# Sparse attention and soft mixture of experts on one core: keys and queries as 128 interleaved rows, first keys in one transfer, strided values in 32 and 4 rows

## The chip, the core and the metric

The kernel runs on one core of one Trainium2 chip. The metric is the device time of one execution in microseconds. One core has five engines that run side by side: the tensor engine (PE, with its weight loads shown apart as PEld), VectorE (DVE), ScalarE (ACT), GpSimd (POOL) and SyncE (SP). SP computes nothing here; it issues nearly all DMA transfers, in the order of the program.

## The reference

```python
def _attn_ref(q, k, v):                       # (8, 8, 576, 64) each: batch, head, row, width
    scores = scale * np.matmul(q, k.transpose(0, 1, 3, 2))
    rel = pos[:, None] - pos[None, :]
    mask_local = (rel >= 0) & (rel < 32)
    mask_strided = (rel >= 0) & (pos[None, :] % 32 == pos[:, None] % 32)
    # heads 0 to 3 local, heads 4 to 7 strided
    attn = softmax of the masked scores over the keys
    return np.matmul(attn, v)

def _moe_ref(x, phi, w1, w2):                 # x (4608, 512), phi (512, 32), w1 (8, 512, 1024), w2 (8, 1024, 512)
    logits = x @ phi
    d = softmax over the 4608 rows;  slot_input = d.T @ x
    for e in range(8): slot_out[e] = np.maximum(slot_input[e] @ w1[e], 0) @ w2[e]
    c = softmax over the 32 slots
    return c @ slot_out
```

The output of attention, heads side by side, is x of the second part.

## The kernel before, in words

Each of the 8 batches has 576 rows, of which 512 (rows 64 to 575) make one set; the first 64 rows of all eight batches make a ninth, the auxiliary set (index B in the code), which is worked fifth. In the list SETS the sets are numbered 0 to 8 in the order of work.

A set goes through named steps. **Loads** (issued by SP): LKl and LQl load keys and queries of the four local heads, LKs and LQs those of the strided heads, into four buffers `ld` (`load_kq`). A buffer has 128 rows of two times 512 elements. A row of the source holds 8 neighbouring positions of one head (2 KB). Before the change, one transfer fills 64 rows of `ld`, with two heads side by side in each row; a second transfer on the other 64 rows brings the other two heads. LDr loads the first 8 source rows of each head's keys (the 64 keys in front of the set) into `rest`, one transfer of 16 KB a head. V1 loads the local heads' values (runs of 256 bytes, two transfers), VS the strided heads' values (two transfers, each to 36 rows with two heads of 4 KB). W1, W2 and W3 load one weight tile of 512 KB (128 rows of 4 KB) each, as long as own buffers are left. The auxiliary set loads in more and smaller transfers.

**On the engines:** TlK, TlQ, TsK, TsQ and Tr transpose keys, queries and first keys on PE (8 transposes each, Tr 4); lK, lQ, sK, sQ, lrK and srK copy the results from PSUM into the operands kbl, ql, kbs and qs, and put them in order on the way. SL and SS are the two score products with their masks; mx, sb, ex and sm the softmax (maximum, subtraction, exponential, sum); V20 to V23 shift values on GpSimd; PTl and PTs transpose the probabilities, AVl and AVs multiply with the values, nl, X, XB and their copies bring both halves into rows and columns; LGl and LGs make the logits, kp keeps them in `lall`; bm, dex, dT, z, SI and acc update the running softmax over rows and the slot inputs.

The order is written out by hand in `ASEQ`: each entry is a step, its stage, and for copies the engine (A is ScalarE, D VectorE). In iteration `it`, a step of stage s works on set `it - s`, so the steps of one set are spread over five iterations, and one iteration has steps of up to five sets. PE, ScalarE and VectorE run in exactly this order; SP issues in the order in which the loads stand in it. A transfer into a buffer waits until the last reader of the old contents is done, and SP, which goes in order, holds everything behind it.

When a step is done for the last set, the buffers that it was the last to read become free for further weight tiles (`alias`, `freed`), 18 in all, and a load for one is put into SP's order at that place. After attention (the end of SI and acc of the last set) come the global softmax weights, the slot inputs, the two expert layers (h, so), the combination weights (`emit_c`, `emit_ct`) and the output, while the remaining weight tiles are loaded and the results stored (the tail). `shape_constants` makes the masks in the row order of the scores.

Of the kernel before, what the change touches and what calls it, by code (L numbers as in the profile page):

```python
# [22 lines left out]
G = 16  # L23
# [23 lines left out]
def shape_constants():  # L47
    q = np.arange(128)

    qq = q % 16 * 2 + q // 16 % 2  # L50
# [27 lines left out]
def tile_sparse_attention_soft_moe(  # L78
# [64 lines left out]
    ql = fix.tile([P, 2, 16, 32], F32, name="ql")  # L143
# [17 lines left out]
    def load_kq(b, x, i):  # L161
        for j in range(2):

            dma = nc.scalar if b == SETS[0] and j else nc.sync
            out = ld[x][i][64 * j:64 * j + 64]
            if b < B:
                dma.dma_start(out=out, in_=rows_of((k, q)[i], b, x, j)[AR:PN])  # L167
                continue
            for a in range(2):
                rows = (k, q)[i][:, 4 * x + 2 * a + j].rearrange("b (p n) d -> b p (n d)", n=TN)  # L170
                nc.sync.dma_start(out=out[:, a], in_=rows[:, 0:AR])  # L171

    def rows_of(src, b, x, j):
        return src[b, 4 * x:4 * x + 4].rearrange("(a j) (p n) d -> j p a (n d)", j=2, n=TN)[j]

    def load_rest(b):

        for h in range(H):
            if b < B:
                nc.sync.dma_start(out=rest[AR * h:AR * h + AR], in_=k[b, h].rearrange("(p n) d -> p (n d)", n=TN)[0:AR])  # L180
# [11 lines left out]
    def load_vs(b):  # L192
        rows = vs.rearrange("p j g d -> p j (g d)")
        for a in range(2):
            if b < B:
                nc.sync.dma_start(out=rows[64 * a:64 * a + NI],
                                  in_=v[b, 4 + 2 * a:6 + 2 * a].rearrange("j (i g) d -> i j (g d)", g=G))
                continue
# [15 lines left out]
    def flat(t, pat, lo):  # L214
        return t.rearrange(pat)[:, lo:lo + 1024]
# [5 lines left out]
    alias += [(flat(ql, "p j t x -> p (j t x)", 0), {"SL"}), (flat(qs, "p n x -> p (n x)", 0), {"SS"})]  # L221
# [73 lines left out]
    def eT(b, x, i, y, cp):  # L295
        tp = bt[b][f"t{x}{i}"]
        tv = tp.rearrange("p a (n r) -> p (a n) r", n=4)
        if x == 1 and i == 1:
            cp(out=qs, in_=tv)
# [554 lines left out]
```

## Time and profile before

| | us |
|---|---|
| median of 3 runs (336.19 to 339.99) | 337.16 |
| the profiled execution | 339.14 |
| its span, from first to last instruction | 337.3 |
| PE busy in it | 253.5 |
| VectorE busy | 171.7 |
| ScalarE busy | 134.1 |
| GpSimd busy | 48.3 |

All durations of the trace are from the profiled execution; its mean granted TensorE clock was 0.842 of full speed. Busy time is the time in which an engine had an instruction running. A DMA share of 1 means that the packets' times add up to the length of the stretch on all 16 DMA engines; as packets overlap on an engine it can be above 1.

### The profile page before, as it was taken

How to read it: one execution, taken by the hardware profiler on the slowest of the kernel's cores; microseconds unless marked ns; L12 is line 12 of the kernel's file. 1: busy time of each engine (PE TensorE's matmuls, PEld its weight loads, DVE VectorE, ACT ScalarE, POOL GpSimd, SP SyncE). 2: the span in 40 equal slices, each digit the busy share in tenths (PEclk: the TensorE clock that was granted, in tenths of full speed). 3: DMA queues.
4: the chain of work that ended last, by engine and by line, in shares of the span. 5: the costliest groups of instructions: out<-in, count | busy, mean ns of one | idle time of the engine just before them, and what ended most of it. 6: DMA issues, size and time to landing. Idle time of an engine off the chain costs nothing.

```text
span 337.3 us, 10114 instructions
## 1 busy us (share of the span) xinstructions
PE 253.5 (75%) x4417; PEld 191.4 (57%) x4417; DVE 171.7 (51%) x316; ACT 134.1 (40%) x235; POOL 48.3 (14%) x47
## 2 busy tenths in 40 slices
PE   7467959779996739886986969995645689999820
PEld 2455847568785638575665848774445343357610
DVE  2157836552865424853861745666103126569740
ACT  1356443633574405544544544452301301128620
POOL 8004004004003000500500400400050002000000
PEclk9789978965999967997898797896759559999985
DMA  6979969969968979978996996999999558999997
GB/s 144 213 168 222 211 154 215 213 153 212 188 192 152 149 157 189 209 182 171 219 204 156 213 212 146 230 266 379 189 277 285 174 187 235 350 347 347 324 343 241
DMA packets 65740, 74.36 MB, mean 220 GB/s; under 512 B 24608, under 2 KB 50592, under 8 KB 65696
## 3 DMA queue, kind: packets, MB, share of 16 engines
q1 hardware_dynamic: 64304, 72.45, 89.2%
q10 hardware_dynamic: 1392, 1.26, 1.5%
q8 instruction: 35, 0.57, 0.8%
q14 instruction: 9, 0.07, 0.1%
HBM read 64.26 MB, written 9.44 MB: 218 GB/s over the span
## 4 chain that ended last, share of the span: by engine, by line
DMA 38%; PE 30%; SPq 10%; DVE 9%; issue 4%; ACT 4%; POOL 1%; ACTq 0%; DVEq 0%; POOLq 0%
DMA wb<-in_moe_w_dram 22%; DMA ld<-in_k_dram 12%; PE h L672 5%; PE so L770 4%; SPq L167 4%; DMA v<-in_v_dram 3%; PE t L293 3%; PE as L280 3%; PE o L798 3%; SPq L187 2%; PE al L280 2%; SPq L171 2%; PE ss L280 2%; DVE kbl L309 2%; PE pt L417 1%
## 5 line engine op out<-in xcount | busy, mean ns | idle before, releaser
L293 PE MATMUL t<-ident,ld 128*128 128x128 f32 x288 | 49.4, 325 | 19.4 <-DMA ld<-in_k_dram 11.1
L293 PEld LDWEIGHTS t<-ident,ld 128*128 128x128 f32 x288 | 40.0, 168 | 26.6 <-issue 14.6
L210 POOL COPY v<-v 32x1024 f32<-32x1024 f32 x18 | 19.1, 1061 | 201.9 <-DMA v<-in_v_dram 155.1
L312 ACT COPY ql<-t 64x512 f32<-64x512 f32 x36 | 20.9, 580 | 36.7 <-PE t L293 31.2
L309 DVE COPY kbl<-t 64x512 f32<-64x512 f32 x18 | 12.4, 688 | 32.1 <-PE t L293 27.1
L280 PE MATMUL as<-pt,vs 36*64 36x32 f32 x1152 | 22.7, 234 | 5.8 <-issue 5.5
L280 PEld LDWEIGHTS as<-pt,vs 36*64 36x64 f32 x1152 | 21.2, 152 | 8.3 <-issue 7.8
L280 PEld LDWEIGHTS al<-v,pt 128*32 128x32 f32 x576 | 17.6, 117 | 11.8 <-POOL v L208 7.0
L280 PE MATMUL al<-v,pt 128*32 128x128 f32 x576 | 19.3, 289 | 6.5 <-POOL v L208 6.1
L302 ACT COPY kbs<-t 64x1024 f32<-64x1024 f32 x18 | 18.1, 1007 | 13.7 <-PE t L293 13.6
L309 ACT COPY kbl<-t 64x512 f32<-64x512 f32 x18 | 10.4, 580 | 30.7 <-DVE kbl L309 30.7
L431 DVE TENSOR_TENSOR xn<-al,rz 128x512 f32<-128x512 f32 x18 | 11.6, 685 | 21.3 <-PE al L280 21.3
L542 ACT COPY pt<-pt 128x1024 f32<-128x1024 f32 x9 | 9.1, 1017 | 27.5 <-PE pt L417 27.5
L208 POOL COPY v<-v 32x1024 f32<-32x1024 f32 x18 | 19.4, 1081 | 1.1
L280 PE MATMUL ss<-kbs,qs 128*32 128x72 f32 x576 | 12.5, 232 | 8.9 <-issue 7.0
L280 PE MATMUL lg<-xt,phs 128*32 128x128 f32 x288 | 15.4, 342 | 4.4 <-issue 3.3
L280 PE MATMUL sl<-kbl,ql 128*32 128x128 f32 x576 | 17.8, 276 | 0.6 <-DVE kbl L336 0.6
L280 PEld LDWEIGHTS sl<-kbl,ql 128*32 128x32 f32 x576 | 15.3, 111 | 4.9 <-DVE kbl L336 1.9
L336 DVE COPY kbl<-tr 64x32 f32<-64x32 f32 x24 | 4.4, 185 | 25.6 <-PE tr L322 18.8
L417 PE MATMUL pt<-ident,pl 128*128 128x128 f32 x72 | 15.6, 387 | 2.1 <-issue 2.1
L543 ACT COPY xt<-as 128x1024 f32<-128x1024 f32 x9 | 9.1, 1013 | 19.9 <-PE lg L280 19.7
L280 PEld LDWEIGHTS ss<-kbs,qs 128*32 128x32 f32 x576 | 10.4, 110 | 11.6 <-issue 11.6
(157 smaller groups left out, 447.4 us busy)
## 6 DMA issues: line engine op xcount, KB each, us to landing
wb<-in_moe_w_dram SPq DMA_DIRECT2D x43, 512.0 KB
ld<-in_q_dram SPq DMA_DIRECT2D x30, 256.0 KB
ld<-in_k_dram SPq DMA_DIRECT2D x30, 256.0 KB
v<-in_v_dram SPq DMA_DIRECT2D x16, 288.0 KB
vs<-in_v_dram SPq DMA_DIRECT2D x16, 288.0 KB
out_dram<-wb SPq DMA_DIRECT2D x6, 512.0 KB
ld<-in_moe_w_dram SPq DMA_DIRECT2D x4, 512.0 KB
v<-in_moe_w_dram SPq DMA_DIRECT2D x3, 512.0 KB
```

The lines of the kernel that those rows point to most:

```text
L167: dma.dma_start(out=out, in_=rows_of((k, q)[i], b, x, j)[AR:PN])
L208: nc.gpsimd.tensor_copy(out=v2[r + 32:r + 64, a], in_=v1[r:r + 32, a, :, 1:9])
L210: nc.gpsimd.tensor_copy(out=v2[r:r + 32, a], in_=v1[r + 32:r + 64, a, :, 0:8])
L280: nc.tensor.matmul(out=out, lhsT=lhsT, rhs=rhs, start=start, stop=stop, skip_group_check=True)
L293: nc.tensor.transpose(out=tp[:, a, P * n:P * n + P], in_=src[:, a, P * n:P * n + P], identity=ident)
L302: cp(out=kbs[r, y].rearrange("p n (j r) -> p n j r", j=2)[:, :, :, AR:PN], in_=tv[r].rearrange("p n (j r) -> p n j r", j=2))
L309: cp(out=kbl[d, a, e::2].rearrange("p n (j r) -> p n j r", j=2)[:, :, :, AR:PN], in_=tp[r, a].rearrange("p (n j r) -> p n j r", n=4, j=2))
L312: cp(out=ql[d, :, :, 16 * e:16 * e + 16].rearrange("p j t (r n) -> p (j t) r n", n=4), in_=tp[r, a].rearrange("p (n t r) -> p t r n", n=4, ...
L417: nc.tensor.transpose(out=ps[:, g // 4, 128 * (g % 4):128 * (g % 4) + 128], in_=(pl[:, 2 * g:2 * g + 2] if x == 0 else psd[:, g]).rearrang ...
L431: nc.vector.tensor_tensor(out=xn[:, :, 0:256].rearrange("p r (a j d) -> p j r a d", a=2, j=2)[:, j], in0=bt[b]["al"][:, j].rearrange("p (r ...
L672: nc.tensor.matmul(out=ph[x][32 * e:32 * e + 32, :], lhsT=sit[:, c, 32 * (4 * g + e):32 * (4 * g + e) + 32], rhs=wts[16 * g + 4 * c + e][: ...
L770: nc.tensor.matmul(out=pos[x][32 * e:32 * e + 32, 0:256], lhsT=hts[g][:, c, 32 * e:32 * e + 32], rhs=wt[:, 256 * e:256 * e + 256], start=( ...
```

## The change

Keys and queries: a transfer now takes two neighbouring heads and fills all 128 rows of one half of `ld`, in the order (row, head), so that row p of head j lands in row 2p + j of the buffer. The evacuations read every second column to sort the heads apart; queries of the local heads are laid out 8 neighbouring rows to a group, SL takes every second column of ql as weights, AVs writes its columns in the same new order, and the logits' rows are put into the old order when they are kept (kp, now two copies), so that the copies of `emit_ct` no longer reorder. The masks follow. The first set's second key and query transfers are issued by SP and no longer by ScalarE. The first keys of all eight heads come in one transfer of 128 KB. The strided values of 36 rows come as rows 4 to 35 and then rows 0 to 3. The free buffers other than `ld` are filled with weight tiles only once V1 and VS of the last set are issued. The order of the steps is a new one; the stages are four higher throughout, which changes nothing by itself.

```diff
 ASEQ = (
-    "V23:4 lK3:3A V22:4 lK2:3D lK0:3A LGs:5 TsQ:3 lrK2:3A lrK3:3D sms:4 W1:4 srK1:3A ePTl:4A nms:4 XB:5 srK0:3A "
-    "kp:5 LDr:2 bm:5 LKl:2 dex:5 eXB:5A SL:3 dT:5 alx:5 sQ:3D edT:5D mxl:3 z:5 TsK:3 sK0:3A SI:5 AVl:4 sbl:3 "
-    "sK1:3A PTs:4 ePTs:4A nl0:4 exl:3 nl1:4 SS:3 mxs:3 sbs:3 LQs:2 acc:5 V1:3 X:4 LKs:2 W2:3 TlQ:2 AVs:4 VS:3 "
-    "Tr:2 lQ0:2A LQl:1 lQ2:2A eX:4D V21:3 exs:3 lQ3:2A LGl:4 sml:3 W3:3 lQ1:2A eAVs:4A TlK:2 lrK0:2D lK1:2D "
-    "lrK1:2D V20:3 PTl:3 "
+    "edT:9D mxl:7 sK1:7A SI:9 sbl:7 sK0:7A PTs:8 SS:7 z:9 ePTs:8A W2:7 nl1:8 nl0:8 W3:8 LKl:6 V1:7 V22:7 X:8 "
+    "acc:9 eX:8A V20:7 mxs:7 Tr:6 lrK0:6A TlK:6 sbs:7 exl:7 lK0:6D lK2:6D lK3:6A lK1:6D LQl:6 AVs:8 LGl:8 LQs:6 "
+    "PTl:7 lrK1:6D V21:7 TlQ:6 LKs:6 exs:7 lQ2:6D eAVs:8A lrK2:6A ePTl:7A lrK3:6D lQ1:6A lQ3:6A lQ0:6A LGs:8 "
+    "LDr:5 sml:7 TsQ:6 XB:8 sQ:6A V23:7 bm:8 W1:7 sms:7 TsK:6 srK0:6A nms:7 kp0:8A kp1:8A SL:6 dex:8 dT:8 VS:7 "
+    "eXB:8A srK1:6A AVl:7 alx:8 "
...
-    qq = q % 16 * 2 + q // 16 % 2
+    qq = q % 4 * 8 + q // 4 % 4 * 2 + q // 16 % 2
...
     def load_kq(b, x, i):
-        for j in range(2):
-            dma = nc.scalar if b == SETS[0] and j else nc.sync
-            out = ld[x][i][64 * j:64 * j + 64]
+        src = (k, q)[i]
+        for a in range(2):
             if b < B:
-                dma.dma_start(out=out, in_=rows_of((k, q)[i], b, x, j)[AR:PN])
+                rows = src[b, 4 * x + 2 * a:4 * x + 2 * a + 2].rearrange("j (p n) d -> p j (n d)", n=TN)
+                nc.sync.dma_start(out=ld[x][i][:, a], in_=rows[AR:PN])
                 continue
-            for a in range(2):
-                rows = (k, q)[i][:, 4 * x + 2 * a + j].rearrange("b (p n) d -> b p (n d)", n=TN)
-                nc.sync.dma_start(out=out[:, a], in_=rows[:, 0:AR])
+            for j in range(2):
+                rows = src[:, 4 * x + 2 * a + j].rearrange("b (p n) d -> b p (n d)", n=TN)
+                nc.sync.dma_start(out=ld[x][i][j::2, a], in_=rows[:, 0:AR])
...
     def load_rest(b):
-        for h in range(H):
-            if b < B:
-                nc.sync.dma_start(out=rest[AR * h:AR * h + AR], in_=k[b, h].rearrange("(p n) d -> p (n d)", n=TN)[0:AR])
+        if b < B:
+            nc.sync.dma_start(out=rest, in_=k[b].rearrange("h (p n) d -> h p (n d)", n=TN)[:, 0:AR])
...
         for a in range(2):
             if b < B:
-                nc.sync.dma_start(out=rows[64 * a:64 * a + NI],
-                                  in_=v[b, 4 + 2 * a:6 + 2 * a].rearrange("j (i g) d -> i j (g d)", g=G))
+                src = v[b, 4 + 2 * a:6 + 2 * a].rearrange("j (i g) d -> i j (g d)", g=G)
+                for lo, hi in ((4, NI), (0, 4)):
+                    nc.sync.dma_start(out=rows[64 * a + lo:64 * a + hi], in_=src[lo:hi])
...
         if x == 1 and i == 1:
-            cp(out=qs, in_=tv)
+            cp(out=qs.rearrange("p n (j r) -> p n j r", j=2), in_=tv.rearrange("p n (r j) -> p n j r", j=2))
         elif x == 1:
...
-               in_=tv[r].rearrange("p n (j r) -> p n j r", j=2))
+               in_=tv[r].rearrange("p n (r j) -> p n j r", j=2))
...
-                   in_=tp[r, a].rearrange("p (n j r) -> p n j r", n=4, j=2))
+                   in_=tp[r, a].rearrange("p (n r j) -> p n j r", n=4, j=2))
...
-                cp(out=ql[d, :, :, 16 * e:16 * e + 16].rearrange("p j t (r n) -> p (j t) r n", n=4),
-                   in_=tp[r, a].rearrange("p (n t r) -> p t r n", n=4, r=4))
+                cp(out=ql[d, :, 32 * e:32 * e + 32].rearrange("p t (n r) -> p t n r", n=4),
+                   in_=tp[r, a].rearrange("p (n t r) -> p t n r", n=4, r=8))
...
-                    mm(ps[32 * c:32 * c + 32, j, 128 * r:128 * r + 128], ql[:, j, 4 * r + c],
+                    mm(ps[32 * c:32 * c + 32, j, 128 * r:128 * r + 128], ql[:, 4 * r + c, j::2],
...
-        pv = ps.rearrange("p a (c e h g) -> p a e g c h", e=2, h=2, g=8)
+        pv = ps.rearrange("p a (t e c h w) -> p a e w c t h", e=2, c=4, h=2, w=2)
...
-    def kp(b):
-        nc.scalar.copy(out=lall[:, SETS[b], :], in_=bt[b]["lg"][:, 0:128])
+    def kp(b, e, cp):
+        cp(out=lall[:, SETS[b], :].rearrange("p (t r n e) -> p e t r n", r=4, n=4, e=2)[:, e],
+           in_=bt[b]["lg"][:, 0:128].rearrange("p (t e n r) -> p e t r n", e=2, n=4, r=4)[:, e])
...
-                for x in [x for x in alias if x[1] <= done]:
+                for x in [x for x in alias if x[1] <= done and ({"V1", "VS"} <= done or x[0].tensor in first)]:
...
-                CTE[vb % 2](out=dst.rearrange("p (c k e) -> p c k e", e=2, k=16),
-                            in_=src.rearrange("p (c e k) -> p c k e", e=2, k=16))
+                CTE[vb % 2](out=dst, in_=src)
```

`first` is the list of the four `ld` buffers.

## Rows read from the trace of the kernel before

**Rows 1.** The page's first two parts, whole span: busy time, share and instructions of each engine; then, in 40 slices of 8.4 us, the share of the DMA engines in tenths and the bytes they moved.

```profile
PE 253.5 (75%) x4417; PEld 191.4 (57%) x4417; DVE 171.7 (51%) x316; ACT 134.1 (40%) x235; POOL 48.3 (14%) x47
...
DMA  6979969969968979978996996999999558999997
GB/s 144 213 168 222 211 154 215 213 153 212 188 192 152 149 157 189 209 182 171 219 204 156 213 212 146 230 266 379 189 277 285 174 187 235 350 347 347 324 343 241
```

**Rows 2.** The page's fourth part: the chain of work that ended last, by engine.

```profile
DMA 38%; PE 30%; SPq 10%; DVE 9%; issue 4%; ACT 4%; POOL 1%; ACTq 0%; DVEq 0%; POOLq 0%
```

**Rows 3.** The timeline of SP, which issues the loads: start, time of the issue, line, what is loaded, how many. The first key loads of set 1 (local heads) and of set 8, and the three weight tiles that go into ld near the end of attention.

```profile
18.06 1.25 SPq L167 DMA_DIRECT2D ld<-in_k_dram  x2
...
205.04 1.25 SPq L167 DMA_DIRECT2D ld<-in_k_dram  x2
...
220.48 5.13 SPq L257 DMA_DIRECT2D ld<-in_moe_w_dram  x3
```

**Rows 4.** Stretches of the span, one row each: from:to, length, busy time and instructions of PE, PE's weight loads, DVE, ACT and POOL, then the granted TensorE clock, the DMA share and GB/s. In order: one set from key load to key load; 3 us around its start; the same around the start of set 8; keys and queries in flight; the last part of the set; weight tiles in flight; the auxiliary set's key and query loads; the tail.

```profile
43.50:69.40 25.90, 18.34 (x397) 14.90 (x397) 12.31 (x22) 11.56 (x19) 4.14 (x4) 0.87 0.95 195
42.50:45.50 3.00, 2.52 (x132) 2.21 (x131) 2.61 (x4) 2.70 (x5) 0.00 (x0) 1.00 0.18 37
204.50:207.50 3.00, 3.00 (x82) 2.67 (x80) 3.00 (x4) 1.02 (x2) 0.00 (x0) 0.64 0.35 89
46.50:51.50 5.00, 1.82 (x9) 1.82 (x10) 0.00 (x0) 1.01 (x1) 0.00 (x0) 0.50 1.09 215
58.60:69.40 10.80, 7.02 (x159) 5.32 (x158) 5.19 (x8) 5.34 (x7) 0.00 (x0) 1.00 0.89 191
228.00:231.00 3.00, 1.21 (x69) 1.21 (x71) 2.93 (x4) 0.56 (x1) 0.00 (x0) 0.92 1.03 402
92.00:94.00 2.00, 1.84 (x42) 1.59 (x46) 1.21 (x2) 0.66 (x1) 0.00 (x0) 1.00 0.55 196
284.00:304.00 20.00, 20.00 (x253) 9.49 (x242) 12.45 (x40) 4.60 (x12) 0.00 (x0) 1.00 1.09 347
```

**Rows 5.** SP's timeline again, the issues of one set, as in rows 3.

```profile
43.84 1.25 SPq L167 DMA_DIRECT2D ld<-in_k_dram  x2
...
49.19 2.92 SPq L167 DMA_DIRECT2D ld<-in_k_dram  x2
52.15 0.60 SPq L257 DMA_DIRECT2D wb<-in_moe_w_dram  x1
52.84 0.75 SPq L196 DMA_DIRECT2D vs<-in_v_dram  x2
...
55.21 2.13 SPq L257 DMA_DIRECT2D wb<-in_moe_w_dram  x2
58.67 10.91 SPq L180 DMA_DIRECT2D rest<-in_k_dram  x8
69.68 1.27 SPq L167 DMA_DIRECT2D ld<-in_k_dram  x2
```

**Rows 6.** The DMA queue's own waits: what SP waited for at line 180 (loads of the first keys), total us, times, longest.

```profile
SPq L180 <- DMA wb<-in_moe_w_dram: 27.4, 17, 3.6
SPq L180 <- DMA vs<-in_v_dram: 17.8, 12, 2.6
```

**Rows 7.** Stretches as in rows 4: the densest 20 us of attention, and all of it up to the end of the last SI.

```profile
80.00:100.00 20.00, 19.35 (x430) 16.05 (x428) 14.04 (x24) 11.89 (x22) 3.69 (x4) 0.91 0.80 199
0.00:269.40 269.40, 203.59 (x3905) 163.30 (x3905) 135.38 (x224) 113.70 (x187) 46.43 (x45) 0.84 0.92 202
```

**Rows 8.** Groups of instructions by line and shape: line, engine, operation, out<-in, shapes, count | busy us, mean ns of one | idle time before them and what ended it. The query and key evacuations of the local heads, the weight loads of the two score products, and the copy of the logits.

```profile
L312 ACT COPY ql<-t 64x512 f32<-64x512 f32 x36 | 20.9, 580 | 36.7 <-PE t L293 31.2 <-DMA ld<-in_k_dram 5.1
...
L280 PEld LDWEIGHTS sl<-kbl,ql 128*32 128x32 f32 x576 | 15.3, 111 | 4.9 <-DVE kbl L336 1.9 <-issue 1.7 <-DVE rz L408 0.8
...
L309 ACT COPY kbl<-t 64x512 f32<-64x512 f32 x18 | 10.4, 580 | 30.7 <-DVE kbl L309 30.7
L280 PEld LDWEIGHTS ss<-kbs,qs 128*32 128x32 f32 x576 | 10.4, 110 | 11.6 <-issue 11.6
...
L495 ACT COPY lall<-lg 128x128 f32<-128x128 f32 x9 | 2.4, 264 | 1.2 <-PE lg L280 1.2
```

**Rows 9.** The chain of work followed back, at the start: start us, us, what.

```profile
2.28 4.74 DMA ld<-in_q_dram
...
7.35 5.92 DMA ld<-in_k_dram
...
13.32 1.98 PE t L293 x8
```

**Rows 10.** The same chain in the last set and after it.

```profile
210.11 1.95 PE t L293 x8
...
233.03 11.33 DMA v<-in_v_dram
...
248.87 3.74 PE al L280 x64
252.61 1.91 PE pt L417 x8
...
269.39 0.76 DVE acc L514
...
292.49 0.86 PE so L770 x16
```

More of the change, by code (lines that the diff above doesn't have):

```diff
@@ L142, in tile_sparse_attention_soft_moe @@
     kbl = fix.tile([P, 2, TN, RW], F32, name="kbl")
-    ql = fix.tile([P, 2, 16, 32], F32, name="ql")
+    ql = fix.tile([P, 16, 64], F32, name="ql")
     kbs = fix.tile([P, 2, 8, RW], F32, name="kbs")
@@ L161, in load_kq @@
     def load_kq(b, x, i):
-        for j in range(2):
-            dma = nc.scalar if b == SETS[0] and j else nc.sync
-            out = ld[x][i][64 * j:64 * j + 64]
+        src = (k, q)[i]
+        for a in range(2):
             if b < B:
-                dma.dma_start(out=out, in_=rows_of((k, q)[i], b, x, j)[AR:PN])
+                rows = src[b, 4 * x + 2 * a:4 * x + 2 * a + 2].rearrange("j (p n) d -> p j (n d)", n=TN)
+                nc.sync.dma_start(out=ld[x][i][:, a], in_=rows[AR:PN])
                 continue
-            for a in range(2):
-                rows = (k, q)[i][:, 4 * x + 2 * a + j].rearrange("b (p n) d -> b p (n d)", n=TN)
-                nc.sync.dma_start(out=out[:, a], in_=rows[:, 0:AR])
-    def rows_of(src, b, x, j):
-        return src[b, 4 * x:4 * x + 4].rearrange("(a j) (p n) d -> j p a (n d)", j=2, n=TN)[j]
+            for j in range(2):
+                rows = src[:, 4 * x + 2 * a + j].rearrange("b (p n) d -> b p (n d)", n=TN)
+                nc.sync.dma_start(out=ld[x][i][j::2, a], in_=rows[:, 0:AR])
     def load_rest(b):
-        for h in range(H):
-            if b < B:
-                nc.sync.dma_start(out=rest[AR * h:AR * h + AR], in_=k[b, h].rearrange("(p n) d -> p (n d)", n=TN)[0:AR])
+        if b < B:
+            nc.sync.dma_start(out=rest, in_=k[b].rearrange("h (p n) d -> h p (n d)", n=TN)[:, 0:AR])
     def load_v1(b):
@@ L220, in tile_sparse_attention_soft_moe @@
              for x in range(2) for i in range(2)]
-    alias += [(flat(ql, "p j t x -> p (j t x)", 0), {"SL"}), (flat(qs, "p n x -> p (n x)", 0), {"SS"})]
+    alias += [(flat(ql, "p t x -> p (t x)", 0), {"SL"}), (flat(qs, "p n x -> p (n x)", 0), {"SS"})]
     alias += [(flat(t, "p e n r -> p (e n r)", x), {n}) for t, n in ((kbl, "SL"), (kbs, "SS")) for x in (0, 1024)]
@@ L446, in AVs @@
                             o = 128 * (2 * e + w) + 32 * c
-                            mm(pv[64 * j:64 * j + 64, a, e, 4 * w + c], vs[d, j, 8 * w + 2 * c + e], pt[d, j, o:o + 32])
+                            mm(pv[64 * j:64 * j + 64, a, e, w, c], vs[d, j, 8 * w + 2 * c + e], pt[d, j, o:o + 32])
     def X(b):
@@ L533, in tile_sparse_attention_soft_moe @@
         "LGl": lambda b: LG(b, 0), "LGs": lambda b: LG(b, 1), "nl0": lambda b: nl(b, 0), "nl1": lambda b: nl(b, 1),
-        "bm": bm, "dex": dex, "alx": alx, "kp": kp, "dT": dT, "z": z, "SI": SI,
+        "bm": bm, "dex": dex, "alx": alx, "dT": dT, "z": z, "SI": SI,
         "acc": lambda b: emit_acc(slice(0, 512), bt[b]["si"], bt[b].get("al_")),
@@ L538, in tile_sparse_attention_soft_moe @@
     moves = {
+        "kp0": lambda b, cp: kp(b, 0, cp), "kp1": lambda b, cp: kp(b, 1, cp),
         "sQ": lambda b, cp: eT(b, 1, 1, 0, cp),
@@ L557, in tile_sparse_attention_soft_moe @@
     done = set()
+    first = [t.tensor for t in ld[0] + ld[1]]
     for it in range(min(x[1] for x in todo), NV + max(x[1] for x in todo)):
```

## The prediction, made before the change was run

> **What bounds the kernel now.** I began with the whole span: tensor engine 75% busy, VectorE and ScalarE about half, the DMA share six to over nine tenths in the first 24 slices (202 us), yet only 144 to 222 GB/s there against about 345 near the end [rows 1]. The chain that ended last is 38% DMA and 10% SP's own issuing [rows 2]. So the larger part of the run waits for loads, and the question is why they are slow there. The unit to look at is one set (one batch's 2.1 MB of keys and queries, 0.13 MB of first keys, 0.59 + 0.59 MB of values, three weight tiles of 0.52 MB, 4.97 MB together). The key loads of set 1 were issued at 18.06 us and those of set 8 at 205.04 [rows 3]: seven sets in 187.0 us, 26.7 us each.
>
> Inside one set I read SP's issues beside the byte rates, and three things show. (1) While only keys and queries move, the rate is 215 GB/s although the DMA share is over 1; where weight tiles alone were queued (the three into ld and those around them), with 128 rows instead of 64, it is 402 GB/s at the same share [rows 3, 4]. The queues are full in both, so I read the 64-row destination as what halves the rate. (2) In the last 10.8 us of the set, which hold two strided value loads, one pair of query loads, two weight tiles and the eight small loads of the first keys, it is 191 GB/s [rows 4]. At their own rates the queries take 2 x 262 KB / 215 = 2.4 us and the two weight tiles 2 x 524 KB / 402 = 2.6; of the 10.8 some 5.8 us are left for the two value loads of 295 KB, 2.9 us each where a weight tile of nearly twice the bytes takes 1.3. (3) The first keys take SP 10.91 us for eight issues of 16 KB [rows 5], since each is held until an earlier load has landed [rows 6]. The last one therefore goes out when everything else is home, and the next keys behind it: in the 3.0 us around that point the rate is 37, in another set 89 GB/s, at DMA shares of 0.18 and 0.35 [rows 4].
>
> The pieces of a set: keys and queries 8 x 1.22 = 9.8 us, strided values 5.8, local values 0.59 MB at the 191 to 215 around them 2.9, weights 3 x 1.30 = 3.9, the hole 3.0 us less what its shares say was busy, 2.0 to 2.5. That is 24.4 to 24.9 of the 25.9 us from one key load to the next, close enough to cost an edit by its piece.
>
> The next bound is the tensor engine. Up to the last SI the trace has 3905 matmuls, 12 of them warm-ups; by nine that is 433 a set [rows 7]. The densest stretch ran 430 in 19.35 us at a granted clock of 0.91 [rows 7]; so 19.5 us a set, with idle time on top.
>
> **The change, part by part.**
>
> *Keys and queries, 128 rows to a transfer.* Same bytes, same eight issues, 2 KB runs as before. If (1) is right they go from 215 to the rate of 128-row loads. Bounds: 215 (no gain, 9.8 us) and 402 (5.2 us). I take 380, for a 2 KB run is half a weight row: 5.5 us, 4.3 less. [...]
>
> *Strided values, 32 + 4 rows.* Two loads become four. The 32 rows are meant to go evenly; the 4 rows carry a ninth of the bytes. Bounds: 5.8 us as now, and 1.5 us at 402. I take 3.0, nearer the lower, since (1) says that the spread of rows is what counts.
>
> *First keys in one transfer.* Removes seven issues a set (23 become 18 with the two extra for values) and, what matters, the hole: one transfer waits for one landing, and later loads queue behind it at once. The transfer is eight heads of 16 KB; the nearest row is the auxiliary set's 128 KB loads, also eight pieces, at 196 GB/s and a share of 0.55 [rows 4]: 0.7 us. The hole of 2.0 to 2.5 us goes. But the new order has waits of its own on SP: V1 for AVl of the set before, at the end of PE's round, with LQl, LQs and LKs behind it; LDr for Tr, with one weight tile and VS behind; VS for AVs, with two weight tiles and the next LKl behind. For a restart after V1's wait I keep 1.5 us (bounds 0 and 3.0).
>
> DMA per set after: 5.5 + 3.0 + 2.9 + 3.9 + 0.7 + 1.5 = 17.5 us (all low ends 14.2; all high ends 26.1). That is below PE's 19.5, so what is late next is PE. With 1.3 us of waits on evacuations and late loads I take 20.4 us for a common set. The auxiliary set stays at 128 KB transfers, sixteen of them at 196: 10.7 instead of 5.5 us, DMA 22.7, so 23 for this one. Mean of seven: (6 x 20.4 + 23) / 7 = 20.8 us (bounds 19.5, PE without a wait, and 26.1, all high DMA ends at once).
>
> *The evacuations that sort.* Reads of every second element from PSUM: the query copies already read in steps and take 580 ns, as the key copies in longer runs do, same size [rows 8]. Nothing, on engines with 12 to 14 us of work in a set [rows 7]. Moving qs and xt to ScalarE and two 64-row copies back keeps both under 15; cover is PE's 19.5. kp becomes two copies, bounded by 0 and one more of 264 ns [rows 8], off the path. Weight loads of every second column of ql: ss already loads so, 110 ns against 111 for sl [rows 8]: nothing. AVs' scattered output columns: no row has a two-column step alone; bounds 0 and a few tenths of a us; I take 0. The closing copies without a step lie beside a tail whose DMA share is 1.09 at 347 GB/s [rows 4]: nothing.
>
> *Start.* Now PE's first key transposes begin at 13.32 us, released by a key load issued at 7.35 behind the first keys [rows 9]. All of set 0's loads then go over SP, 0.6 us an issue for 262 KB as now [rows 3]. One transfer and two key loads, 0.66 MB, come first; ScalarE's query load, issued at 2.28 among others, was home 4.74 us later [rows 9]; a key load issued at 1.5 in the same crowd is there at 6 us (bounds 4.8 and 10.3). Less 7.3.
>
> *Last set.* Now V1 of set 8 sits on SP behind weight tiles that fill freed buffers: issued at 233.03, 11.33 us to land, and AVl starts at 248.87 [rows 10]. From set 8's key transposes (210.11) to the end of the last SI (269.4) it is 59.3 us. Afterwards only the tiles into ld go ahead; the others wait for V1 and VS. At the new pace: 15.5, three quarters of 20.4, for the rest of set 8's round; 3 for LQl and LKs, which now stand on SP behind ld tiles that wait for TlK and TlQ; 15.5 again for the next round, which has no key and query transposes and no sl; 17 for the closing chain (now from AVl's end, 252.6, to 269.4): 51 us (bounds 46 and 59). The eleven tiles now held back cost 11 x 1.3 = 14 us of DMA, first needed by so at 292.49, 23 us after SI [rows 10]: covered; without that cover it would be up to 14 us.
>
> *Tail.* From acc to the end, 67.9 us, full of DMA and PE, is left alone (bounds -1, +3).
>
> **The sum.** Now 13.3 + 9.8 (to set 1's place) + 187.0 + 59.3 + 67.9 = 337.3. After: 6 + 9.8 + 7 x 20.8 + 51 + 67.9 = 280.3. The profiled execution took 339.14, 1.84 more than its span, and the median of the runs is 0.994 of it: (280.3 + 1.84) x 0.994 = 280.5, so 280 us.
>
> **The rivals.**
>
> *A: the rate stays at that of 64 rows.* What speaks for it: no load in the trace pairs a 128-row destination with a source of 64 rows by two heads, and the slow rate could come from the 2 KB runs. Against: the auxiliary loads have 2 KB runs too and give 196 GB/s at half the share. [...] Time: 4.3 us more DMA a set, 21.8 + 1.3 = 23.1, with slower start (8) and end (54): 8 + 9.8 + 161.7 + 54 + 67.9 = 301.4, 301 us.
>
> *B: the hole comes back at V1.* SP waits in order; V1 for AVl, and TlQ, TsQ, TsK then need LQl, LQs, LKs within the first half of PE's round. For: the strided heads' key loads, issued next after V1, held SP for 2.92 us where a free pair takes 1.25 [rows 5]. Against: LKl is ahead of V1, and six loads at 0.7 us are quick. If PE stands 3 us a set, 23.8: 280.3 + 21 = 301 us.
>
> *C: slower, fewer engines.* A transfer whose source steps between two heads may be spread over few engines, as the share of 0.55 hints for the auxiliary set's eight pieces [rows 4]. Price: with x GB/s for 2.1 MB, a set is slower than 26.7 once keys and queries take 26.7 - 12.0 = 14.7 us, below 143 GB/s. At a quarter of 196 they take 43 us, a set 55, and the run 530 us. The auxiliary loads, eight pieces at 196, speak against falling that far.
>
> **How the numbers follow.** Forecast 0.64, A 0.16, B 0.14, C 0.03, and 0.03 for other outcomes near today's time (a later wait eats all). The range takes in 19.5 us a set with the best start and end (5 + 9.8 + 136.5 + 46 + 67 = 264) and A and B at 301, with half of their 21 us again to spare for the size of either: 264 to 312. The three runs of before lie within 1.1%, so about 1% is what can be told from no change. Faster by over 1%: 0.64 + 0.16 + 0.14 + 0.01 = 0.95; within 1% 0.02; slower 0.03.
>
> **What would show it.** In the trace after: stretches of key and query loads alone above 340 GB/s (A: near 215); one first-key issue a set, of under a us, and no 3 us stretch under 100 GB/s between sets; a set of 20 to 21.5 us with PE busy over 90%, clock near 1; first key transposes near 6 us; set 8's V1 issued right after the AVl before it; 68 us from the last SI to the end. Wrong if PE idles for loads in every set (B), if the clock drops below the 0.91 of the dense stretch (1 us more a set per 5%), or if the tail grows since the held-back tiles are late.

## The result, and the profile after

The changed kernel takes 287.83 us (median; 287.54 to 290.65), the kernel before 337.58 beside it: a ratio of 0.854, with a 95% interval of 0.847 to 0.861. Predicted were 280, with a range of 264 to 312. The profiled execution has a span of 285.6 us where the sum said 280.3. Here and below, ratios leave out executions that are over 1.5% longer than the fastest of the same kernel, medians and ranges do not.

The page of the changed kernel: busy time of the engines; PE's granted clock and the DMA share in 40 slices of 7.1 us; then the chain of work that ended last, by engine.

```profile
PE 238.1 (83%) x4417; PEld 175.3 (61%) x4417; DVE 156.8 (55%) x308; ACT 141.2 (49%) x252; POOL 46.9 (16%) x47
...
PEclk9999789999999975999978699999965699999965
DMA  7999999699878998879979919976999999999997
...
PE 65%; DVE 7%; issue 7%; ACT 7%; DMA 6%; SPq 4%; DVEq 0%; ACTq 0%
```

Against [rows 1, 2]: DMA has gone from 38% of the chain to 6%, SP's own issuing from 10 to 4, PE from 30 to 65. The same matmuls keep PE busy for 15 us less; its mean clock rose from 0.842 to 0.902. The bound has moved, as forecast. But the DMA engines are hardly less busy than before: still at nine tenths in most slices of attention.

The same chain in order of time (start, us, what), which dates each step of the sum: the first key transposes; `sl` of sets 1, 2, 3, 5, 6, 7 and 8 (the auxiliary one is not on the chain); what the chain went through in the auxiliary set; two of PE's pauses ("issue": PE waits for nothing that the profile shows); set 8's key transposes, the AVl of sets 7 and 8, and acc after the last SI.

```profile
5.92 1.19 PE t L289 x8
...
25.14 2.48 PE sl L276 x66
...
50.32 2.32 PE sl L276 x66
...
70.60 2.32 PE sl L276 x66
...
92.64 10.80 DMA ld<-in_k_dram
...
118.18 2.32 PE sl L276 x66
...
136.66 2.32 PE sl L276 x66
...
140.67 2.53 issue
...
153.72 3.17 issue
...
165.20 2.32 PE sl L276 x66
...
174.44 1.02 PE t L289 x8
...
184.45 2.31 PE sl L276 x66
187.03 2.07 PE al L276 x64
...
199.52 1.88 PE al L276 x64
...
217.61 0.76 DVE acc L512
```

From one `sl` to the next: 25.2, 20.3, 47.6 for the auxiliary set and its neighbour together, 18.5, 28.5, 19.3. Three of the five common sets run at or under the 20.4 us forecast for one, the other two don't; the mean of seven is 22.8 instead of 20.8. That is where the prediction was off.

Stretches of the changed kernel, columns as in [rows 4]: seven sets from `sl` to `sl`; keys and queries in flight; the strided values with weight tiles; a set without a pause; the set with two of them.

```profile
25.14:184.29 159.15, 140.22 (x3019) 114.19 (x3019) 90.99 (x164) 91.97 (x155) 28.96 (x28) 0.91 0.90 231
...
40.00:42.00 2.00, 2.00 (x113) 1.83 (x112) 1.36 (x2) 1.17 (x3) 1.88 (x3) 1.00 1.05 389
...
44.00:50.00 6.00, 4.44 (x48) 3.84 (x49) 3.12 (x8) 4.09 (x8) 0.00 (x0) 1.00 1.05 210
...
118.18:136.66 18.48, 18.37 (x434) 15.17 (x433) 13.20 (x25) 13.38 (x25) 4.14 (x4) 1.00 0.84 224
136.66:165.20 28.54, 22.74 (x434) 17.98 (x433) 13.22 (x25) 13.36 (x25) 4.14 (x4) 0.82 0.92 236
```

Keys and queries move at 389 GB/s where [rows 4] had 215. The stretch with the strided values still shows 210 at a DMA share of 1.05. And the first row holds the difference to the forecast: in a set PE is busy for 140.22 / 7 = 20.0 us and idle for 2.7, where the forecast for a common set had 19.5 and 0.9.

What PE waited for in these seven sets (total us, times, longest):

```profile
PE al L276 <- issue: 7.3, 3, 3.4
PE t L289 <- DMA ld<-in_k_dram: 3.7, 2, 2.2
PE lg L276 <- issue: 3.2, 1, 3.2
...
PE t L289 <- DMA ld<-in_q_dram: 0.9, 2, 0.6
```

With 1.5 and 1.0 us before two other steps the pauses make 13.0 of the 18.9 us, the waits for loads 4.6. All of these 4.6 stand in the auxiliary set and its neighbour, between 84.67 and 103.58. In the five common sets PE waited for no load: the one without a pause in the rows above took 18.5 us, the one with two 28.5, 5.7 of it in the pauses and 4.4 more in matmuls at a granted clock of 0.82 instead of 1.00.

SP's timeline (columns as in [rows 3]): the one load of the first keys and the four of the strided values, in one set.

```profile
39.67 0.64 SPq L175 DMA_DIRECT2D rest<-in_k_dram  x1
...
42.54 2.23 SPq L193 DMA_DIRECT2D vs<-in_v_dram  x4
```

And SP's longest wait: total us, times, longest.

```profile
SPq L182 <- PE al L276: 36.4, 7, 9.9
```

0.64 us of SP instead of 10.91 [rows 5]. SP now waits for PE, at V1, 5.2 us a set.

### The profile page after: what moved, and what is told of

Read it like the earlier page. It is cut to its first block, busy times and chain, and to the rows that moved or that the text cites. A ratio compares the mean times of both kernels' runs of the same rounds, so it can differ in the third digit from the quotient of the medians.

```text
span 285.6 us, 10033 instructions
## 1 busy us (share of the span) xinstructions
PE 238.1 (83%) x4417; PEld 175.3 (61%) x4417; DVE 156.8 (55%) x308; ACT 141.2 (49%) x252; POOL 46.9 (16%) x47
## 4 chain that ended last, share of the span: by engine, by line
PE 65%; DVE 7%; issue 7%; ACT 7%; DMA 6%; SPq 4%; DVEq 0%; ACTq 0%
PE t L289 7%; PE sl L276 7%; PE as L276 6%; PE al L276 6%; PE pt L413 6%; PE h L673 5%; PE so L769 5%; ACT ql L308 4%; DMA ld<-in_k_dram 4%; PE ss L276 4%; PE o L797 3%; SPq L170 3%; PE lg L276 3%; PE si L276 3%; PE x L449 3%
## 5 line engine op out<-in xcount | busy, mean ns | idle before, releaser
L289 PE MATMUL t<-ident,ld 128*128 128x128 f32 x288 | 42.9, 288 | 7.9 <-DMA ld<-in_k_dram 4.3
L289 PEld LDWEIGHTS t<-ident,ld 128*128 128x128 f32 x288 | 32.6, 146 | 15.6 <-issue 3.4
L305 DVE COPY kbl<-t 64x512 f32<-64x512 f32 x27 | 18.5, 686 | 19.6 <-PE t L289 13.1
L276 PE MATMUL al<-v,pt 128*32 128x128 f32 x576 | 18.9, 276 | 7.3 <-issue 7.3
L276 PEld LDWEIGHTS al<-v,pt 128*32 128x32 f32 x576 | 15.7, 110 | 9.1 <-issue 8.1
L308 DVE COPY ql<-t 64x512 f32<-64x512 f32 x9 | 6.2, 684 | 24.4 <-PE t L289 24.4
L308 ACT COPY ql<-t 64x512 f32<-64x512 f32 x27 | 15.7, 581 | 5.3 <-DVE ql L308 5.0
L539 ACT COPY xt<-x 128x1024 f32<-128x1024 f32 x9 | 9.1, 1012 | 13.6 <-PE x L449 13.6
L384 DVE TENSOR_REDUCE mx<-sl 128x16 f32<-128x1024 f32 x9 | 11.0, 1217 | 5.3 <-PE sl L276 5.3
L673 PE MATMUL h<-wb,v 128*32 128x512 f32 x104 | 13.8, 637 | 0.0
L276 PEld LDWEIGHTS lg<-xt,phs 128*32 128x32 f32 x288 | 7.7, 114 | 9.9 <-issue 7.5
```

Of the source, the lines that this page charges most:

```text
L276: nc.tensor.matmul(out=out, lhsT=lhsT, rhs=rhs, start=start, stop=stop, skip_group_check=True)
L289: nc.tensor.transpose(out=tp[:, a, P * n:P * n + P], in_=src[:, a, P * n:P * n + P], identity=ident)
L305: cp(out=kbl[d, a, e::2].rearrange("p n (j r) -> p n j r", j=2)[:, :, :, AR:PN], in_=tp[r, a].rearrange("p (n r j) -> p n j r", n=4, j=2))
L308: cp(out=ql[d, :, 32 * e:32 * e + 32].rearrange("p t (n r) -> p t n r", n=4), in_=tp[r, a].rearrange("p (n t r) -> p t n r", n=4, r=8))
L384: nc.vector.tensor_reduce(out=stats(b, "mx", x), in_=scores(b, x), op=ALU.max, axis=AX.X)
L673: nc.tensor.matmul(out=ph[x][32 * e:32 * e + 32, :], lhsT=sit[:, c, 32 * (4 * g + e):32 * (4 * g + e) + 32], rhs=wts[16 * g + 4 * c + e][: ...
```

## The experiments

The theory at the start was the prediction's own: in the old kernel each piece of a set's DMA time is on the path, so each part of the change gives its piece until PE binds. The rival: the DMA engines are the bound as a whole, so that filling a hole gives nothing, and a part counts once another has moved the bound. Times of different experiments are compared through their ratios to the kernel before, which ran beside each. Of four kernels (the rows alone, all but the rows, and in the new kernel the values in 36 rows and the old rule for buffers) only the times are used.

**The first keys in one transfer, alone, in the old kernel.**

```diff
-        for h in range(H):
-            if b < B:
-                nc.sync.dma_start(out=rest[AR * h:AR * h + AR], in_=k[b, h]...[0:AR])
+        if b < B:
+            nc.sync.dma_start(out=rest, in_=k[b].rearrange("h (p n) d -> h p (n d)", n=TN)[:, 0:AR])
```

> The kernel before with one edit: the first keys of all eight heads in one transfer (everything else as before). My theory: the hole of 2.0 to 2.5 us a set, in which nothing is in flight, goes, in seven sets and at the start, where the key load no longer stands behind eight small ones: 337 falls to 314 to 322 us, and the 3 us around a set's first key load move at 150 GB/s or more instead of 37 to 104. Rival (the hole is only moved, since SP goes in order and the next wait takes its place): 330 to 338 us.

Measured 338.48 us, ratio 0.996 (0.990 to 1.001): nothing, though the hole is gone. One set of this kernel, from one set's first key load to the next, columns as in [rows 4]:

```profile
42.26:68.34 26.08, 23.33 (x496) 18.93 (x496) 14.77 (x25) 14.25 (x22) 4.14 (x4) 0.91 1.02 182
```

In this set the share went from 0.95 [rows 4] to 1.02, and the bytes from 195 to 182 GB/s: more packet time, and no more moved. So the 3 us at 37 and 89 GB/s were real, but filling them gained nothing there. Why is not settled. The chain of this run is not that of the kernel before [rows 2]:

```profile
PE 47%; DMA 25%; issue 8%; SPq 6%; ACT 5%; DVE 5%; ACTq 0%; DVEq 0%
```

DMA and SP have fallen from 48% of it to 31, PE and its pauses have risen from 34 to 55. Less was waited for loads, and as much came back in PE's work and pauses.

**The strided values in 32 and 4 rows, alone, in the old kernel.**

```diff
-                nc.sync.dma_start(out=rows[64 * a:64 * a + NI], in_=v[b, ...]...)
+                src = v[b, 4 + 2 * a:6 + 2 * a].rearrange("j (i g) d -> i j (g d)", g=G)
+                for lo, hi in ((4, NI), (0, 4)):
+                    nc.sync.dma_start(out=rows[64 * a + lo:64 * a + hi], in_=src[lo:hi])
```

> The kernel before with one edit: strided values as 32 rows (4 to 35) and 4 rows (0 to 3). My theory (the spread of the rows sets the rate, not the bytes): 2.8 us less DMA a set where DMA is the bound, 337 falls to 312 to 320 us. Rival (value rows cost by their bytes and by the issue, of which there are now two more a set): 335 to 340 us.

333.33 us, ratio 0.984 (0.974 to 0.993): 5.5 us over the run (2 to 9 by the interval), where 2.8 us a set would have been some 20.

**The 128-row keys and queries with what they need, without the other parts.** The old order, first keys, values and rule for freed buffers are kept.

> The kernel after, with the old order of steps, the old eight loads of the first keys, the old 36-row values and the old rule for freed buffers; so of the change only the 128-row keys and queries with the sorting copies are left. My theory: 4.3 us less DMA a set, 337 falls to 298 to 308 us, and keys and queries alone move at 380 to 400 GB/s. Rival (the gain came from the hole and the order): 325 to 335 us.

312.94 us, ratio 0.916 (0.910 to 0.923). Of the change's 49 us (0.146 of 338) the rows give 28 alone.

**All but the 128-row keys and queries.** The new order, first keys, values and rule, with 64-row loads and the old copies.

> The kernel after without the 128-row keys and queries: old 64-row transfers and old copies, with the new order, one transfer for the first keys, 32 + 4 value rows and the new rule for freed buffers. My theory (rival A of the prediction as an experiment): DMA is 4.3 us a set longer, 21.8 us, and again about as long as PE's round: 300 to 306 us. Rival (order and hole did it, the rate of the rows hardly matters): 287 to 293 us.

318.07 us, ratio 0.937 (0.931 to 0.943): the rows are worth 28 us inside the new kernel (0.937 less 0.854, of 338). That is more than the 300 to 306 us that the price of rival A gave.

**The new kernel with one part undone**, four runs. Eight first-key loads:

> The kernel after, with the eight loads of 16 KB for the first keys again. One transfer alone changed nothing in the kernel before, so two readings are open. One: the hole was never worth anything, since the loads around it slow down by as much when it is filled; then 286 to 291 us here. Two: it was worth nothing only while DMA was the bound in every other microsecond of the set; now that PE sets the pace, eight issues that each wait for a landing hold up the loads behind them: 296 to 306 us, with SP's first-key issues at 5 us or more a set.

299.33 us, ratio 0.886 (0.879 to 0.893). The edit that gave nothing in the old kernel is worth 0.032 of 338, 11 us, in the new one. The values in one transfer of 36 rows:

> The kernel after, with the strided values in two transfers of 36 rows again. In the kernel before the split was worth 1.6%, some 0.7 us a set. If the split still only saves DMA time that PE's round now covers: 287 to 290 us. If the values are the loads that a set waits for: 293 to 300 us.

292.13 us (286.16 to 294.41): its fastest run lies under the fastest of the changed kernel, 287.54, so no worth of this part is shown in the new kernel. The old order of steps:

> The kernel after, with the old order of steps (kp in its two halves on ScalarE at the old place); loads as after. If the loads alone made the gain: 287 to 295 us. If the order is needed so that PE does not wait for a load that SP issued late: 302 to 312 us, near the 313 of the 128-row loads alone.

292.68 us, ratio 0.868 (0.859 to 0.877), about 5 us, though the intervals just touch. The old rule for freed buffers:

```diff
-                for x in [x for x in alias if x[1] <= done and ({"V1", "VS"} <= done or x[0].tensor in first)]:
+                for x in [x for x in alias if x[1] <= done]:
```

> The kernel after, with the old rule for freed buffers: weight tiles go into them at once, ahead of V1 and VS of the last set. My theory (8 us of the prediction's last set hang on it): SP's V1 of set 8 comes 5 to 10 us later and the run takes 293 to 298 us. Rival (buffers free themselves too late to get ahead of V1 in the new order): 287 to 290 us.

299.95 us (294.78 to 302.96), ratio 0.878 (0.863 to 0.894): 8 us by the ratios, 3 to 14 by its interval, 1 to 16 with that of the changed kernel too.

Undone one by one in the new kernel, the parts sum to 28 + 11 + 5 + 8 = 52 us, with nothing shown for the values; those made alone in the old one to 0 + 5.5 + 28 = 34 (the order and the rule were not tried there); together they gave 49. The first keys show that a part's worth depends on the kernel around it: nothing in the old one, 11 us in the new. That fits the rival theory, but its reason, that full DMA engines made the hole worthless, is argued and not shown. It leaves open why the new kernel's sets are longer than PE's work.

**How fast a load of each shape is.** Loads only, block by block, nothing else.

> Loads alone, all computation left out, twelve blocks one behind the other, each of eight to sixteen transfers, so that the rate of a shape can be read undisturbed. Theory P (the partitions that a transfer writes set its rate; each group of neighbouring partitions has one way in): 64 partitions in a row 215 to 230 GB/s whichever half, 128 partitions 380 to 400, every second partition of 128 (the same source and 64 rows) near the 128-row rate, 340 or more; value rows 4 to 35 and rows 0 to 31 alike and at about 215; rows 0 to 3 alone below 60 GB/s; the whole 36 rows and 32 + 4 alike, 110 to 200, since the four rows are what they are slow for either way. Theory S (the source's pattern of two heads or the count of 64 rows sets it): every second partition stays at 215 to 230. Theory V (the unevenness of 36 over the engines was the cost, the one my prediction used): rows 4 to 35 and 32 + 4 both above 300, 36 near 200.

The columns are as in [rows 4], for VectorE and GpSimd alone: from:to, length, busy times, then clock, DMA share, GB/s. In order: 64 rows (halves in turn); the best 2 us of every second row of 128, that is 64 rows spread out; rows 0 to 63 each time; values, 36 rows; values, 32 and 4; values, rows 4 to 35; rows 0 to 31; rows 0 to 3; weight tiles.

```profile
28.00:32.00 4.00, 0.00 (x0) 0.00 (x0) 1.00 1.06 237
...
59.30:61.30 2.00, 0.00 (x0) 0.00 (x0) 1.00 0.86 322
...
72.00:76.00 4.00, 0.00 (x0) 0.00 (x0) 1.00 1.06 200
...
89.00:93.00 4.00, 0.00 (x0) 0.00 (x0) 1.00 0.77 198
...
108.00:112.00 4.00, 0.00 (x0) 0.00 (x0) 1.00 0.97 149
...
131.00:135.00 4.00, 0.00 (x0) 0.00 (x0) 1.00 0.99 220
...
146.00:151.00 5.00, 0.00 (x0) 0.00 (x0) 1.00 0.92 206
158.00:162.00 4.00, 0.00 (x0) 0.00 (x0) 1.00 0.24 57
170.00:174.00 4.00, 0.00 (x0) 0.00 (x0) 1.00 1.01 412
```

And, from the trace's landings, the time from one transfer's landing to the next (the median where nothing else is said: the two wide kinds have two or three gaps of 1.1 to 1.9 us in a block, whose cause was not found, and a mean of 0.95 and 0.96):

| transfer | us | |
|---|---|---|
| 256 KB to 64 rows, halves in turn | 1.09 | 1.00 in a second block |
| 256 KB to 64 rows, always 0 to 63 | 1.32 | |
| 256 KB to 128 rows | 0.68 | SP issues one in 0.65; 0.67 in a second block |
| 256 KB to every second row of 128 | 0.66 | SP issues one in 0.65 |
| 288 KB of values to 36 rows (mean) | 1.53 | |
| the same as 32 + 4 rows (mean) | 1.89 | |
| 256 KB of values to rows 4 to 35 (mean) | 1.12 | |
| 32 KB of values to rows 0 to 3 (mean) | 0.56 | |

64 rows of the same source go as fast as 128 when they are spread over all the rows, and slower by 1.5 to 2 times when they are neighbours (1.1 to 1.3 times by the means, 1.04 to 1.25 against 0.96, which take the gaps in). Over 4 us the neighbours get 200 and 237 GB/s at a DMA share of 1.06, the spread rows 322 in the best 2 us. So it is neither the number of rows nor the source's two heads: in these blocks it is where the 64 rows lie among the 128. And 32 neighbours (220, 206 GB/s) are no better than 64 (237, 200): that 32 rows divide evenly, on which my 3.0 us rested, brings nothing by itself. Split off, the four rows are slow (57 GB/s), and by themselves the two transfers are slower than the one (1.89 against 1.53).

Of the three theories P came nearest. Its reason, one way in for each group of neighbouring rows, is shown by no run. The values stay at half the 412 GB/s of the weight tiles or under it, in either form: 198 in 36 rows, 149 in 32 and 4.

**What a set's loads need with nothing else running.** Loads only, in the new order of loads, three sets of each of six kinds.

> Loads alone, all computation and all waits for buffers left out: six blocks of three sets each in the new order of loads, with 64-row keys and queries, 36-row values, eight first-key loads; then with one first-key load; then with 32 + 4 value rows too; then 128-row keys and queries with 36 rows; with 32 + 4 rows; with 32 + 4 rows and eight first-key loads. My prediction's terms give 22 us a set for the first (without the hole), 21 to 22 for the second, 19 for the third, 17.5 for the fourth, 15 for the fifth (its 17.5 less the restart and with local values at full rate 14.5), and 0 to 1 more for the sixth. If the value split gives the transfers nothing, the third is as the second and the fifth as the fourth; if it gives what the first experiment on it showed, 1 to 1.7 us less.

Columns as above; each of the first six rows goes from the last landing of a block's first set to that of its third, two sets. 64 rows with 36-row values and eight first-key loads; with one; with 32 + 4 as well; 128 rows with 36; with 32 + 4; with 32 + 4 and eight first-key loads. Then, inside one set of the fourth kind, six key and query loads; the three weight tiles with the two strided value loads; and the same with 32 + 4 rows, from the fifth.

```profile
31.47:78.90 47.43, 19.35 (x16) 0.00 (x0) 1.00 0.96 210
102.88:152.11 49.23, 12.54 (x11) 0.00 (x0) 1.00 1.04 205
175.56:223.32 47.76, 12.72 (x11) 0.00 (x0) 1.00 1.05 209
243.01:283.86 40.85, 12.94 (x10) 0.00 (x0) 1.00 1.06 243
306.42:346.16 39.74, 12.94 (x10) 0.00 (x0) 1.00 1.04 252
366.76:408.12 41.36, 12.30 (x10) 0.00 (x0) 1.00 0.94 240
...
246.44:250.34 3.90, 0.76 (x1) 0.00 (x0) 1.00 0.98 345
250.95:260.36 9.41, 1.66 (x2) 0.00 (x0) 1.00 1.05 235
314.69:323.58 8.89, 1.66 (x2) 0.00 (x0) 1.00 1.03 240
```

A set's loads take 23.7, 24.6, 23.9 us with 64-row keys and 20.4, 19.9, 20.7 with 128. This is the row that the prediction lacked. It had 16.0 us of loads (17.5 with its restart); in this run they take 19.9 with no buffer to wait for, as long as PE's 20.0. One or eight first-key loads make no difference of a constant sign, so the hole is no piece of the time of loads alone. Within the set, six 128-row loads take 0.65 us each, as forecast, and weights and strided values 9.4, where their times alone add up to 7.0 (3 x 1.30 + 2 x 1.53). If the three weight tiles keep their 1.30 [rows 4], 5.5 us are left for the values, 5.0 in the split form.

**Half of the auxiliary set's key and query loads on ScalarE's queue.**

```diff
-                nc.sync.dma_start(out=ld[x][i][j::2, a], in_=rows[:, 0:AR])
+                (nc.sync, nc.scalar)[j].dma_start(out=ld[x][i][j::2, a], in_=rows[:, 0:AR])
```

> The changed kernel with half of the auxiliary set's sixteen key and query issues on ScalarE's queue. If that set is long because SP issues its sixteen transfers one after another (10.7 us in the trace of after), about 5 us of these go: 283 us, ratio to before 0.84. If the set waits for something else (its landing, the tensor engine), 287 to 288; if ScalarE's issues hold up its copies, 289 to 292.

292.19 us, ratio 0.857 (0.848 to 0.867): no gain. From the last V1 before the auxiliary set to the first one after it, two sets, it is 52.0 us (47.6 in the changed kernel). ScalarE's issues stand in the order of its copies and came late (from 79.03 us on). Eleven transfers of 128 KB then land between 89.65 and 96.66 us, 0.70 apart, though two queues issue them. That is the spacing in the changed kernel with SP alone (82.83 to 88.20, nine landings, 0.67 apart, from issues 0.64 apart), where 4 us of them show, columns as in [rows 4]:

```profile
82.00:86.00 4.00, 3.69 (x90) 2.99 (x83) 1.05 (x2) 3.05 (x4) 3.10 (x3) 1.00 0.54 200
```

But the two queues issued these eleven between 84.22 and 92.97, 0.88 apart, no faster than SP alone. So the run does not tell what a quicker second issuer would give. While such transfers, of eight pieces each, are in flight the DMA share is 0.54 here and 0.55 in [rows 4]; why it stays near half was not found.

**The changed kernel with the strided values loaded for the first set alone.**

```diff
     def load_vs(b):
+        if b != SETS[0]:
+            return
```

> The changed kernel with the strided values loaded for the first set alone (later sets multiply with the first set's values, and the strided half of the output follows from that). This takes the 5.0 to 5.5 us that these loads took among the others in the run of loads alone out of each set's 20 us, and changes no instruction of the tensor engine. Theory E (in the changed kernel loads and tensor engine need about the same 20 us a set, and each waits for the other's hiccups; my prediction had the loads at 17.5 and so covered): sets fall to 20 to 20.5 us, the auxiliary pair from 47 to 43, the total to 268 to 275. Theory F (the loads are covered, as predicted, and the sets are long for the tensor engine's own pauses for instructions and the auxiliary set's landings): 283 to 288. In between, 276 to 282, both count.

278.53 us (276.89 to 281.83), ratio 0.819 (0.815 to 0.822): 9 us by the medians, 12 by the ratios, between the two theories. The trace is that of the longest of its runs, 281.83. Its seven sets from `sl` to `sl`, columns as in [rows 4], and then the later of these starts on its chain, in order of time:

```profile
26.09:173.52 147.43, 137.18 (x3018) 113.59 (x3018) 90.54 (x163) 91.57 (x153) 28.96 (x28) 0.93 0.78 230
```

```profile
51.17 2.32 PE sl L278 x66
...
72.15 2.32 PE sl L278 x66
...
111.32 2.32 PE sl L278 x66
...
131.10 2.32 PE sl L278 x66
...
152.65 2.32 PE sl L278 x66
...
173.68 2.32 PE sl L278 x66
```

PE's idle time in the seven sets falls from 18.9 to 10.3 us. Its waits for loads are 4.6 us in the changed kernel and 3.8 here; what fell are the pauses, from 13.0 to 5.7. The auxiliary pair takes 39.2 us (47.6), with waits for loads of 1.8 instead of 4.6 and a granted clock of 1.00 instead of 0.89; the others take 25.1, 21.0, 19.8, 21.6 and 21.0. The one of 28.5 is gone, but none is shorter than the 18.5 and 19.3 that two sets of the changed kernel took with all their loads. So the strided loads cost 9 to 12 us of the run, but not, as theory E has it, through PE waiting for loads in every set: those waits are in the auxiliary pair, and one of 2.0 us in the first set here. Theory F had the pauses right and the gain too small.

What the pauses wait for can be read in the packets, though no run took it away. The changed kernel has six of 1.4 us or more up to the last SI, 14.5 us together. Each ends 1.3 to 1.7 us after the end of a 16 KB transfer of instructions: the pause of 140.67 to 143.20 after one that ended at 141.79, that of 153.72 to 156.89 after one that ended at 155.23. In the traces of the kernel before, the first keys alone, the values alone, the eight first-key loads, the old order and the two queues, every PE pause of this kind of 1 us or more ends so too: with the six, 56 in seven traces, 1.2 to 1.9 us behind such an end. By chance that would hold for about one in twelve, as 35 such transfers lie in 285.6 us. So PE seems to stand there for instructions; the other 29 transfers of the changed kernel have no such pause behind them. Whether a pause comes when data hold the instructions up, so that fewer loads make fewer pauses, or by luck of the execution, stays open: there is one trace of each kernel.

Three of the five pauses of 1.4 us or more in the seven sets of the changed kernel cost twice. The granted clock is at half (0.50 of full speed) from 31.7 to 38.5, 103.3 to 113.6, 144.3 to 147.7 and 154.5 to 161.4 us, 27 us together, each time in or right after a pause (3.4, 2.5 and 3.2 us) or the wait of 2.2 us for a key load. Behind the pauses of 1.5 and 1.4 us, which end at 45.45 and 54.74, it stays at 1.00.

## Why the prediction was right, and which terms were off

By its own sum, the profiled execution gives: first key transposes at 5.92 (forecast 6); from there to set 8's 168.5, where 9.8 + 7 x 20.8 = 155.4 was forecast, 13.1 more; from 174.44 to the end of SI at 217.6 it is 43.2 (51), 7.8 less; the tail 68.0 (67.9). Together 5.3 us over. The remaining 2.5 are mostly the median, which stands at 1.000 of the profiled execution, not at 0.994, and half a us of rounding.

- *The bound.* Right: DMA is 6% of the chain, PE 65%, and in common sets PE waited for no load.
- *Keys and queries.* Right: 380 GB/s forecast, 389 in the trace. The reading of (1), that the destination decides, is what the run of loads alone shows; rival A is out. "128 rows instead of 64" was loose: 64 spread rows do as well, 256 KB in 0.66 us against 0.68.
- *Strided values.* Wrong: 3.0 us forecast, 5.0 to 5.5 left for them among the other loads. The step that failed is the choice between the bounds of 5.8 and 1.5, "nearer the lower, since (1) says that the spread of rows is what counts". (1) says the contrary: 32 neighbours don't spread, and alone they went at 206 and 220 GB/s.
- *First keys.* The load itself was priced at its least: 0.7 forecast, 0.6 in one set of the loads alone (from 250.34 to 250.95 in the fourth block), 0.8 to 1.5 in the other five sets of the fourth and fifth blocks. The hole as "2.0 to 2.5 us" of a set's DMA time is wrong for the old kernel (0 us) and, at some 11 us over the run, a little over half right for the new one.
- *DMA per set.* Forecast 16.0 and a restart of 1.5. The second set of the fourth block took 19.6: local values 3.4 (forecast 2.9), keys and queries 6.1 (5.5; the two behind the weight tiles take 1.1 each), first keys 0.6, weights 3.9, strided values 5.5 (3.0). So the term is too short by some 4 us, and the 2 us by which the forecast had PE cover the loads don't exist. It cost little here: the sets were stretched by PE's pauses, so by this run the loads still had 2.9 us to spare in a mean set of 22.8, and PE waited 4.6 us for them in all seven.
- *PE per set.* (168.5 - 9.8) / 7 = 22.7 instead of 20.8, seven times: this is the term that was off. The forecast's seven sets hold 136.5 us of PE at work and 9.1 idle, the trace 140.2 and 18.9. The missing piece is the pauses, 13.0 us, which the prediction put at nothing although "issue" is 4% of the chain in [rows 2], some 13 us of that run; without them the idle time is 5.9 and the 9.1 would have been ample. The sum also has a slip: 19.5 and "1.3 us of waits" are 20.8 and not 20.4, and with that the mean would have been 21.1 and the forecast some 2 us higher.
- *The auxiliary set.* 23 forecast; with its neighbour 47.6, against 43.4. Its key and query loads go at 200 GB/s, as read from [rows 4]; the pair is long by PE's 4.6 us of waits for them and for the neighbour's keys (issued at 92.64, landed 10.8 us later), 0.9 of pause, and 10 us at half the clock behind.
- *A restart after V1's wait, rival B.* SP waits 5.2 us a set at V1, but for a PE that has its data; the share over the seven sets is 0.90, from which I estimate that some 2 us of a set are free of transfers, near the 1.5 kept. It is no hole as in B: in common sets PE waited for no load.
- *The sorting evacuations, the split kp, AVs' columns.* Right at nothing: the query copies take 581 ns (580), AVs' matmuls 228 (234 in the kernel before), the two kp copies 225 each, 0.19 us more a set than the one of 264 [rows 8], off the path.
- *Last set.* Too long by 7.8: from AVl of set 7 (end 189.10) to that of set 8 (201.40) the trace has 12.3, where 3 + 15.5 was set. The 3 us for LQl and LKs behind the tiles into ld did not come, and the round without transposes is shorter than "15.5 again". Of the forecast for this part the rule that holds the tiles back is worth about 8 us (1 to 16).
- *Clock.* The prediction named a clock below 0.91 as what would make it wrong. It was 0.91 over the seven sets: 1.00 in a set without a pause, 0.82 in the one with two.

So the forecast case came true with two errors of opposite sign, +13 and -8; that 280 came within 3% of 287.83 is in part luck. The first could have been smaller, since the row was to be had: [rows 2] showed PE's pauses on the chain. A second row was at hand as well: [rows 4] showed 191 GB/s with a share of 0.89 for a mix of loads, and I priced the change from loads that ran alone.

## What to carry to other kernels

Look at where a transfer's rows lie, not at how evenly they divide: 64 rows spread over the 128 landed 256 KB every 0.66 us, 64 neighbours every 1.00 to 1.32. Interleaving two heads over 128 rows took keys from 215 to 389 GB/s, while 32 and 4 neighbours in place of 36 gave 5.5 us in the old kernel and nothing shown in the new one. Filling the hole at the first keys was worth nothing in the old kernel and 11 us in the new one, so parts are to be tried in the kernel in which they will run. Before calling loads covered, add up their time in the mix in which they run: 19.9 us, not 16.0. And before calling an engine the bound, give its pauses a term: here 13 us in seven sets, and 17 us at half the clock in or behind three of them.

## What the runs showed of the hardware

64 rows at every second of 128 land 256 KB every 0.66 us (SP issues one in 0.65), 64 neighbours every 1.0 to 1.3. Four rows of values alone get 57 GB/s with a DMA share of 0.24. Two strided value loads and three weight tiles, 7.0 us by their times alone, take 9.4 together; why was not found. A DMA share above 1 went with anything from 182 to 412 GB/s, so it does not tell how many bytes move. PE's pauses of 1 us or more for which the profile shows no cause end 1.2 to 1.9 us after the end of a 16 KB transfer of instructions, 56 of 56 in seven traces.
